# Dilated attention, then routed experts, on one core: query blocks of 64 with two heads in the halves of the array, routing of two batches at a time, and place writes that are not ordered among themselves

## The chip, the cores and the metric

The kernel runs on one core of one Trainium2 chip. The metric is device time in microseconds (us). Three runs of the kernel before gave 985.47, 986.65 and 988.72 us; the median, 986.65 us, is the time before. About 0.3% (3 us) is what a measurement of this kernel can tell from no change.

## What is computed

Eight batches of 576 positions, eight heads of 64 features. A head attends over a causal window: heads 0 to 3 over the last 32 positions, heads 4 to 7 over every fourth of the last 128. The result, with the heads side by side, is x with 512 features per token. Each token has the logits of eight experts and a local gate; where the gate is at least one half, the token takes the expert of the token before it, otherwise that of its largest logit. The expert is two matmuls with a ReLU between.

```python
scores = where(mask, q @ k.T / 8, -1e9);  attn = softmax(scores);  x = attn @ v       # mask by head
logits = x @ w_gate;  local_gate = sigmoid(x @ w_local)
e = argmax(logits[b, s]) if s == 0 or local_gate[b, s] < 0.5 else prev_e               # in order of s
out[b, s] = softmax(logits[b, s])[e] * (relu(x[b, s] @ w1[e]) @ w2[e])                 # w1 512x1024, w2 1024x512
```

## The kernel before

Everything is float32, and each float32 matmul of the program is two passes in the profile. The dilated heads are stored by position modulo 4, so that both kinds of head have a window of 32 neighbours.

**Attention.** The loop over n runs over 32 pairs of heads (four per batch). `scores(n)` (L227) takes six blocks of 96 queries against 128 keys. The two heads of a pair share one matmul of 128 rows: the host lays q out with zeros (`_apart`, L656), 192 columns for a block, so that each head's 64 features meet zeros of the other. VectorE adds the mask out of PSUM (L241), ScalarE takes the exponential (L244). `values(n)` (L277) multiplies the 12 blocks of weights with v, whose last column of ones gives the sums, and VectorE normalises into `x` of the batch (L290 to L292).

**Routing.** After a batch's four pairs `route(b)` (L579) puts nine steps into the list `waiting`; `gap()` runs one of them at each of three places of the loop. They store x to the array `xd` in DRAM (L302, L307), turn x by TensorE (`x_turn`, L317) into `xt`, make the logits (L332, four column tiles of the array side by side), choose the expert (`fresh`, `carry`, `carry_over`, `carry_in`, `choose`) and, in `place` (L429), give each token a place in the table `tab` in DRAM. Eight indirect DMAs of GpSimd (L447) write the pairs of token and gate, `pay`, to the places `pi`, 72 tokens at a time. These write to the same tensor, and the framework orders each behind the one before it. The small tiles of the routing come from a pool of two buffers, and `pay` is written by L426 and L427.

**Experts.** The tokens of an expert fill tiles of 128; there are 43 tiles in all. The first 8 are planned by `table(False)` after five batches, the others by `table(True)` after all eight. A tile gathers its x (`gather`, L539), turns it (`features`, L546, L548), and runs `hidden` (L557, L559) and `output` (L565, L567); L568 scatters the result to the tokens' rows. w1 and w2 of an expert (2 MB each) go into two slots, tile t into slot t % 2, by a conditional load on SyncE's queue (L534) where the expert of tile t differs from that of tile t - 2. `tokens(True)` (L512) is called at tile 5 and needs all of `tab`. The routing of the last batch runs in the gaps of the first tiles.

What sets the order: TensorE runs in the order in which the program is written; the other engines' order is a scheduler's, and each of them works strictly in that order. SyncE issues the loads of q, k, v, the stores of x and the weights, on one queue. GpSimd issues the place writes, the gathers and the result's scatters, on another.

Of the kernel before, what the change touches and what calls it, by code (L numbers as in the profile page):

```python
# [10 lines left out]
F32 = mybir.dt.float32  # L11
BF16 = mybir.dt.bfloat16
I32 = mybir.dt.int32
Act = mybir.ActivationFunctionType
Alu = mybir.AluOpType
AX = mybir.AxisListType
ET = mybir.EngineType
PSUM = bass.MemoryType.PSUM
# [12 lines left out]
QB = 96  # L31
NB = S // QB
KW = QB + WIN
HB = NB // 2

NP = H // 2
UB = 2
NU = NB // UB
VW = DH + 1

TB = 72
NJ = S // TB
NC = 4
LW = 32
# [4 lines left out]
FLOOR = 2.0 ** -100  # L49
CEIL = 80.0 * DH ** 0.5  # L50
# [7 lines left out]


EARLY, FIRST = 5, 8  # L60
assert EARLY * S - E * (P - 1) > (FIRST - 1) * P
# [13 lines left out]
C_TOK = C_CODE + NJ  # L75
C_ROW = C_TOK + NJ
C_COL = C_ROW + NT
C_ALL = C_COL + 1


def constants():

    c = np.zeros((P, C_ALL), np.float32)
    c[:, C_ID:C_TRI] = np.eye(P)
    c[:TB, C_TRI:C_IDX] = np.triu(np.ones((TB, TB)), 1)
    c[:, C_IDX:C_REV] = np.arange(E)
    c[:, C_REV:C_BASE] = E - np.arange(E)
    c[:, C_BASE:C_CODE] = np.arange(E) * CAP * P
    s = np.arange(NJ)[None] * TB + np.arange(P)[:, None]
    c[:, C_CODE:C_TOK] = s * CW + E  # L90
    c[:, C_TOK:C_ROW] = s
    c[:, C_ROW:C_COL] = np.arange(NT)
    c[:, C_COL] = np.arange(P)
    return c


def block_mask(edge=None):

    p = np.arange(QB)[:, None]
    w = np.arange(KW)[None]  # L100
    ok = (w > p) & (w <= p + WIN)
    if edge is not None:
        ok &= ~((p >= edge) & (w - WIN < edge))
    return np.where(ok, 0.0, MASK)


def masks():

    plain = [block_mask(0)] + [block_mask()] * (NB - 1)
    starts = {i // QB: i % QB for i in range(0, S, CI)}  # L110
    dilated = [block_mask(starts.get(i)) for i in range(NB)]
    return np.concatenate([m.T for m in plain + dilated], 1).astype(ml_dtypes.bfloat16)


def query_masks():

    plain = [block_mask(0)] + [block_mask()] * (NB - 1)
    starts = {i // QB: i % QB for i in range(0, S, CI)}
    dilated = [block_mask(starts.get(i)) for i in range(NB)]
    return np.concatenate([np.eye(QB)] + plain + dilated, 1).astype(ml_dtypes.bfloat16)  # L120
# [3 lines left out]
def dilated_attn_locality_moe_kernel(  # L124
    ctx: ExitStack,
    tc: tile.TileContext,
    q: bass.AP,
    k: bass.AP,
# [13 lines left out]
    ones = keep.tile([QB, P], F32, name="ones")  # L142
# [3 lines left out]
    args = (q, k, v, wgl, w1, w2, con, msk, qmk, out, cst, wg, ones)  # L146
# [9 lines left out]
def whole(ctx, tc, exact, bad, q, k, v, wgl, w1, w2, con, msk, qmk, out, cst, wg, ones):  # L156
# [8 lines left out]
    xd = dram.tile([N + 1, D], F32, name="xd")  # L165
    tab = dram.tile([(PADS + 1) * P, 2], F32, name="tab")
    ident = cst[:, C_ID:C_TRI]

    once = pool("once", 1)
    ins = pool("ins", 3)  # L170
    work = pool("work", 6)
    xp = pool("xp", 2)
    sm = pool("sm", 2)
    gp = pool("gp", 3)
    mp = pool("mp", 2)
    banks = pool("banks", 6, space=PSUM)
    pvp = pool("pvp", 1, space=PSUM)

# [5 lines left out]
    rec = once.tile([QB, B * NP, 2, NB], F32, name="rec")  # L184
    loaded = {}

    def load(n):
        qt = ins.tile([P, NB, 2, QB], F32, name="qt")
        kt = ins.tile([P, WIN + S], F32, name="kt")
        vt = ins.tile([P, 2, NB, VW], F32, name="vt")  # L190
        nc.sync.dma_start(out=kt, in_=k[n])
        nc.sync.dma_start(out=qt.rearrange("p i u s -> p (i u s)"), in_=q[n])
        nc.sync.dma_start(out=vt.rearrange("p u i e -> p (u i e)"), in_=v[n])
        loaded[n] = kt, qt, vt

    load(0)
    if not exact:
        mk = once.tile([KW, 2 * NB * QB], BF16, name="mk")
        nc.sync.dma_start(out=mk, in_=msk)
    else:  # L200
        qm = once.tile([QB, QB + 2 * NB * KW], BF16, name="qm")
# [7 lines left out]
    fill = once.tile([P, PADS + 1, 2], F32, name="fill")  # L209
    nc.vector.memset(fill[:, :, 0], NOBODY)  # L210
    nc.vector.memset(fill[:, :, 1], 0.0)
    nc.gpsimd.dma_start(out=tab.rearrange("(p r) c -> p (r c)", p=P), in_=fill.rearrange("p r c -> p (r c)"))
    zero = once.tile([1, D], F32, name="zero")
    nc.vector.memset(zero, 0.0)
    nc.gpsimd.dma_start(out=xd[N:N + 1], in_=zero)
# [3 lines left out]
    def load_first():  # L219

        for i in range(2):
            nc.sync.dma_start(out=w1s[i].rearrange("p m k f -> p (m k f)"), in_=w1[0])
            nc.sync.dma_start(out=w2s[i].rearrange("p m f -> p (m f)"), in_=w2[0])
# [3 lines left out]
    def scores(n):  # L227
# [4 lines left out]
        for c in range(NU):  # L232
            sc = bank([KW, 2, UB, QB], "sc")
            for i in range(UB):
                s = (c * UB + i) * QB
                nc.tensor.matmul(sc[:, :, i], lhsT=kt[:, s:s + KW], rhs=qt[:, c * UB + i],  # L236
                                 start=True, stop=True)
            pr = work.tile([KW, 2, UB, QB], F32, name="pr")
            at = (kind * NB + c * UB) * QB
            flat = pr.rearrange("w u i p -> w u (i p)")  # L240
            nc.vector.scalar_tensor_tensor(  # L241
                flat, sc.rearrange("w u i p -> w u (i p)"), CEIL,
                mk[:, at:at + UB * QB].unsqueeze(1).to_broadcast([KW, 2, UB * QB]), Alu.min, Alu.add)
            nc.scalar.activation(pr, pr, Act.Exp, scale=SCALE)  # L244
            prob[n].append(pr)

    def scores_exact(n):
# [4 lines left out]
        for c in range(NU):  # L252
            sc = bank([QB, UB, 2, KW], "sc")
            first = True
            for i in range(UB):
                s = (c * UB + i) * QB
                at = QB + (kind * NB + c * UB + i) * KW
                for u in range(2):
                    nc.tensor.matmul(sc[:, i, u], lhsT=qm[:, :QB], rhs=qm[:, at:at + KW],
                                     start=first, stop=False, skip_group_check=True)  # L260
                    nc.tensor.matmul(sc[:, i, u], lhsT=qt[:, c * UB + i, u], rhs=kt[:, s:s + KW],
                                     start=False, stop=True, skip_group_check=True)
                    first = False
            top = sm.tile([QB, UB, 2], F32, name="top")
            nc.vector.tensor_reduce(top, sc, axis=AX.X, op=Alu.max, negate=True)
            nc.vector.tensor_scalar_mul(top, top, SCALE)
            ex = work.tile([QB, UB, 2, KW], F32, name="exq", bufs=1)
            pt = bank([KW, 2, UB, QB], "pt")
            for i in range(UB):
                for u in range(2):  # L270
                    nc.scalar.activation(ex[:, i, u], sc[:, i, u], Act.Exp, scale=SCALE, bias=top[:, i, u:u + 1])
                    nc.tensor.transpose(pt[:, u, i], ex[:, i, u], ident[:QB, :QB])
            pr = work.tile([KW, 2, UB, QB], F32, name="pr")
            nc.vector.tensor_copy(pr, pt)
            prob[n].append(pr)

    def values(n, u):  # L277
        b, g = divmod(n, NP)
        vt = loaded[n][2]
        if g == 0 and u == 0:  # L280
            xs[b] = xp.tile([QB, NB, D], F32, name="x")
        if u == 0:
            prob[n].append(pvp.tile([QB, 2, 512], F32, name="pv"))
        ps = prob[n]
        pv = ps[NU][:, :, :NB * VW].rearrange("p u (i e) -> p u i e", i=NB)
        for i in range(NB):
# [410 lines left out]
```

## Time and profile before

| | before |
|---|---|
| runs, median (lowest to highest) | 986.65 us (985.47 to 988.72) |
| profiled execution, own time | 981.2 us |
| its span | 979.0 us |
| TensorE busy | 817.4 us (84%) |
| VectorE busy | 202.0 us (21%) |
| ScalarE / GpSimd busy | 131.3 us (13%) / 148.3 us (15%) |
| bytes moved by DMA | 165.88 MB |

The span runs from the first to the last instruction of the core; 2.2 us of the profiled execution lie outside it. Busy shares are means over a stage of attention, some 325 us, and a stage of experts, the rest, which have different limits. The chain of waits follows the last instruction back to what released each step, so that a wait on it has cost time, and a busy engine off it has not.

### The profile page before, as it was taken

How to read it: one execution, taken by the hardware profiler on the slowest of the kernel's cores; microseconds unless marked ns; L12 is line 12 of the kernel's file. 1: busy time of each engine (PE TensorE's matmuls, PEld its weight loads, DVE VectorE, ACT ScalarE, POOL GpSimd, SP SyncE). 2: the span in 40 equal slices, each digit the busy share in tenths (PEclk: the TensorE clock that was granted, in tenths of full speed). 3: DMA queues.
4: the chain of work that ended last, by engine and by line, in shares of the span. 5: the costliest groups of instructions: out<-in, count | busy, mean ns of one | idle time of the engine just before them, and what ended most of it. 6: DMA issues, size and time to landing. Idle time of an engine off the chain costs nothing.

```text
span 979.0 us, 13125 instructions
## 1 busy us (share of the span) xinstructions
PE 817.4 (84%) x5310; PEld 641.2 (65%) x5310; DVE 202.0 (21%) x639; ACT 131.3 (13%) x263; POOL 148.3 (15%) x158
## 2 busy tenths in 40 slices
PE   6981728283562999599999999999999999999995
PEld 6880628273562776376776777677677677677764
DVE  4561405252433213001001010010100100101000
ACT  2430303030331100000000000000000000000000
POOL 0011111111123222211111111111111111111000
PEclk9995858695977799889999999999999999999998
DMA  8875767482842166558885281731381370820000
GB/s 299 298 225 178 254 212 210 130 214 56 255 92 60 36 212 202 188 192 324 332 320 209 103 306 44 284 124 43 119 291 35 129 284 33 317 99 33 31 1 4
DMA packets 39637, 165.88 MB, mean 169 GB/s; under 512 B 6904, under 2 KB 16391, under 8 KB 33936
## 3 DMA queue, kind: packets, MB, share of 16 engines
q1 hardware_dynamic: 30448, 143.84, 43.3%
q0 software_dynamic: 9120, 21.11, 6.7%
q8 instruction: 44, 0.72, 0.3%
q14 instruction: 25, 0.20, 0.1%
HBM read 242.18 MB, written 21.04 MB: 269 GB/s over the span
## 4 chain that ended last, share of the span: by engine, by line
PE 66%; DMA 26%; issue 4%; DVE 2%; POOL 1%; SPq 0%; POOLq 0%; DVEq 0%
PE hp L557 30%; PE yp L565 29%; DMA tab<-pay,pi 25%; PE sc L236 2%; PE pv L287 2%; PE tp L546 2%; DMA qt<-in_q_dram 1%; POOL tab L447 1%; DVE pr L241 0%; PE tp L317 0%; POOL xg L539 0%; PE kp L437 0%; DVE x L292 0%; DMA tr_late<-tab,ri_late 0%; PE lp L332 0%
## 5 line engine op out<-in xcount | busy, mean ns | idle before, releaser
L557 PEld LDWEIGHTS hp<-xgt,w1s 128*128 128x128 f32 x2752 | 317.5, 194 | 20.2 <-issue 18.2
L557 PE MATMUL hp<-xgt,w1s 128*128 128x128 f32 x2752 | 319.1, 277 | 1.2 <-DVE xgt L548 1.2
L565 PE MATMUL yp<-w2s,h 128*128 128x512 f32 x688 | 302.4, 592 | 0.0
L565 PEld LDWEIGHTS yp<-w2s,h 128*128 128x128 f32 x688 | 127.4, 190 | 144.0 <-issue 144.0
L559 ACT ACTIVATE h<-hp 128x512 f32<-128x512 f32 x86 | 51.4, 597 | 599.4 <-PE hp L557 599.4
L236 PE MATMUL sc<-qt,kt 128*128 128x192 f32 x384 | 86.5, 386 | 25.5 <-DMA qt<-in_q_dram 25.5
L447 POOL DMA_INDIRECT tab<-pay,pi x64 | 59.8, 934 | 308.1 <-DMA tab<-pay,pi 221.0
L236 PEld LDWEIGHTS sc<-qt,kt 128*128 128x128 f32 x384 | 77.2, 229 | 27.7 <-issue 27.6
L567 DVE TENSOR_SCALAR y<-yp,gate 128x512 f32<-128x512 f32 x43 | 32.2, 750 | 271.3 <-PE yp L565 271.3
L568 POOL DMA_INDIRECT out_dram<-y,tok x43 | 43.3, 1006 | 293.5 <-DVE y L567 266.2
L548 DVE COPY xgt<-tp 128x512 f32<-128x512 f32 x43 | 29.7, 690 | 273.1 <-PE tp L546 273.1
L437 PE MATMUL kp<-cum,ones 72*72 72x64 f32 x16 | 3.6, 326 | 96.2 <-DVE cum L415 96.2
L287 PE MATMUL pv<-vt,pr 128*96 128x65 f32 x768 | 78.2, 256 | 0.0
L244 ACT ACTIVATE pr<-pr 128x384 f32<-128x384 f32 x96 | 48.4, 523 | 217.5 <-DVE pr L241 111.1
L287 PEld LDWEIGHTS pv<-vt,pr 128*96 128x96 f32 x768 | 74.8, 173 | 0.4
L539 POOL DMA_INDIRECT xg<-xd,tok x43 | 41.9, 975 | 215.0 <-PE tp L546 199.1
L437 PEld LDWEIGHTS kp<-cum,ones 72*72 72x72 f32 x16 | 2.3, 199 | 97.2 <-DVE cum L415 97.2
L241 DVE SCALAR_TENSOR_TENSOR pr<-sc,mk 128x384 f32<-128x384 f32 x96 | 50.4, 551 | 27.8 <-PE sc L236 18.8
L292 DVE TENSOR_TENSOR x<-pv,rec 96x768 f32<-96x768 f32 x32 | 30.4, 951 | 1.1 <-DVE rec L291 0.4
L546 PE MATMUL tp<-cst,xg 128*128 128x128 f32 x172 | 26.3, 276 | 0.0
L426 DVE TENSOR_SCALAR pay<-cst 72x8 f32<-72x8 f32 x8 | 1.2, 166 | 110.6 <-DMA tab<-pay,pi 110.6
L546 PEld LDWEIGHTS tp<-cst,xg 128*128 128x128 f32 x172 | 20.4, 143 | 0.0
(118 smaller groups left out, 189.4 us busy)
## 6 DMA issues: line engine op xcount, KB each, us to landing
w1s<-in_w_dram SPq DMA_DIRECT2D x45, 2048.0 KB
w2s<-in_w_dram SPq DMA_DIRECT2D x45, 2048.0 KB
qt<-in_q_dram SPq DMA_DIRECT2D x32, 576.0 KB
vt<-in_v_dram SPq DMA_DIRECT2D x32, 390.0 KB
kt<-in_k_dram SPq DMA_DIRECT2D x32, 304.0 KB
xd<-x SPq DMA_DIRECT2D x8, 576.0 KB
xd<-x SPq DMA_DIRECT2D x16, 192.0 KB
xd<-x SPq DMA_DIRECT2D x16, 96.0 KB
```

The lines of the kernel that those rows point to most:

```text
L236: nc.tensor.matmul(sc[:, :, i], lhsT=kt[:, s:s + KW], rhs=qt[:, c * UB + i], start=True, stop=True)
L241: nc.vector.scalar_tensor_tensor(flat, sc.rearrange("w u i p -> w u (i p)"), CEIL, mk[:, at:at + UB * QB].unsqueeze(1).to_broadcast([KW, 2 ...
L244: nc.scalar.activation(pr, pr, Act.Exp, scale=SCALE)
L287: nc.tensor.matmul(pv[:, u, i], lhsT=ps[i // UB][:, u, i % UB], rhs=vt[:, u, i], start=True, stop=True)
L447: nc.gpsimd.indirect_dma_start(out=tab, out_offset=bass.IndirectOffsetOnAxis(ap=pi[:, j:j + 1], axis=0), in_=st["pay"][:, j], in_offset=None)
L539: nc.gpsimd.indirect_dma_start(out=x, out_offset=None, in_=xd if t >= FIRST else xd[:EARLY * S], in_offset=bass.IndirectOffsetOnAxis(ap=of ...
L546: nc.tensor.transpose(tp[:, kk], x[:, kk * P:(kk + 1) * P], ident)
L557: nc.tensor.matmul(hp[:, m], lhsT=w1s[t % 2][:, half * FK // 2 + m, kk], rhs=x[:, kk], start=(kk == 0), stop=(kk == DK - 1))
L559: nc.scalar.activation(ht[t][:, half * FK // 2:(half + 1) * FK // 2], hp, Act.Relu)
L565: nc.tensor.matmul(yp, lhsT=h[:, m], rhs=w2s[t % 2][:, m], start=(m == 0), stop=(m == FK - 1))
L567: nc.vector.tensor_scalar(y, yp, of_tile("gate", t), None, Alu.mult)
L568: nc.gpsimd.indirect_dma_start(out=out, out_offset=bass.IndirectOffsetOnAxis(ap=of_tile("tok", t), axis=0), in_=y, in_offset=None, bounds_ ...
```

## The change

Query blocks are of 64 (nine of them, against 96 keys). q and k come unpadded, in one array and one load per pair. A score matmul has 64 rows: head u of the pair stands in rows 64u to 64u+63 of the array (`tile_position=(u * DH, 0)`) and writes a PSUM bank of its own. A value matmul has 64 columns: head u stands in columns 64u to 64u+63 (`(0, u * QB)`), so that the result has two heads' queries on 128 partitions. VectorE works on units of five and four blocks. The floor under the sums is gone, and the clamp of the scores is done with the mask in the same instruction (maximum, then minimum, where it was minimum, then add).

```diff
-        for c in range(NU):
-            sc = bank([KW, 2, UB, QB], "sc")
...
-                nc.tensor.matmul(sc[:, :, i], lhsT=kt[:, s:s + KW], rhs=qt[:, c * UB + i],
-                                 start=True, stop=True)
+        for a, z in UNITS:
+            sc = scp.tile([P, 2, 512], F32, name="sc")
+            for i in range(a, z):
+                for u in range(2):
+                    h = slice(u * DH, (u + 1) * DH)
+                    nc.tensor.matmul(sc[:KW, u, (i - a) * QB:(i - a + 1) * QB], lhsT=kt[h, i * QB:i * QB + KW],
+                                     rhs=qt[h, i * QB:(i + 1) * QB], start=True, stop=True,
+                                     tile_position=(u * DH, 0))
...
+                    nc.tensor.matmul(pv[u * QB:(u + 1) * QB, i - a], lhsT=pr[:, u, (i - a) * QB:(i - a + 1) * QB],
+                                     rhs=vt[:, u, i], start=True, stop=True, tile_position=(0, u * QB),
+                                     skip_group_check=True)
```

x is kept per two pairs (256 features of a batch) and turned by `turn(m)` in nine transposes of 128. Routing takes two batches at a time: four routes instead of eight, 96 tokens by 12 instead of 72 by 8, seven steps, two gaps per pair. The running count of each expert is one scan instead of eight additions. `pay` lies in the constants, one row of buffers per route, and `pi` has two buffers. The twelve place writes of a route are declared free of order among all place writes; the reads of `tab` wait for all of them.

```diff
-        st["pay"] = pay = sm.tile([TB, NJ, 2], F32, name="pay")
-        nc.vector.tensor_scalar(pay[:, :, 0], cst[:TB, C_TOK:C_ROW], float(b * S), None, Alu.add)
-        nc.vector.tensor_tensor(pay[:, :, 1], mine, total, op=Alu.mult)
+        nc.vector.tensor_tensor(pay[:, g, :, 1], mine, total, op=Alu.mult)
...
-        for j in range(NJ):
-            nc.gpsimd.indirect_dma_start(
+            i = nc.gpsimd.indirect_dma_start(
                 out=tab, out_offset=bass.IndirectOffsetOnAxis(ap=pi[:, j:j + 1], axis=0),
-                in_=st["pay"][:, j], in_offset=None)
+                in_=pay[:, g, j], in_offset=None)
+            for other in scatters:
+                tc.declare_no_dep(i.ins, other.ins, reason="no two tokens have one place")
+            scatters.append(i)
```

x goes to two arrays, `xd[0]` for the plain heads and `xd[1]` for the dilated ones, 128 features (512 bytes) in a piece; a tile gathers two halves, by `tok` and by a third column `pos` of the table. The stores of the first four batches are issued as their tiles are done, the others after the last pairs. Eleven tiles are planned early (from four batches) instead of eight (from five), so that the tiles' order of experts is another; `tokens(True)` is called at tile 8. The experts' tiles take over the memory of the attention's pools, and `tokens(False)` with the first gathers is called behind the last pair instead of two pairs ahead of it. The first weights are loaded at pairs 22 and 25 (slot 0) and 31 (slot 1) instead of all at pair 12.

```diff
+        b, g = divmod(m, 2)
+        to = xd[g][b * S:(b + 1) * S].rearrange("(i q) (u f) -> u q i f", q=QB, u=2)
+        for u in range(2):
+            nc.sync.dma_start(out=to[u], in_=x[u * QB:(u + 1) * QB].rearrange("q i g d -> q i (g d)"))
...
-EARLY, FIRST = 5, 8
+EARLY, FIRST = 2, 11
...
-        if n == 3 * NP:
-            load_first()
-        if n == B * NP - 2:
-            tokens(False)
...
+        if n == NPB - 2:
+            for m in range(KEPT, (n - 1) // 2):
+                store(m)
+        if n in (NPB - 10, NPB - 7):
+            load_first(0, n > NPB - 9)
+        if n == NPB - 1:
+            load_first(1, False)
+            load_first(1, True)
+    for m in sorted(xs):
+        store(m)
+    attention.close()
...
+    tokens(False)
```

Three places show what moves. GpSimd, the place writes (DMASW0 to DMASW7 are the eight semaphores that its DMAs take in turn; a row with none waits for no DMA). Before:

```order
L447 DMA tab<-pay,pi 36992x2 [waits DMASW0_49,DVE_49]
L447 DMA tab<-pay,pi 36992x2 [waits DMASW2_49]
L447 DMA tab<-pay,pi 36992x2 [waits DMASW3_49]
L447 DMA tab<-pay,pi 36992x2 [waits DMASW4_49]
L447 DMA tab<-pay,pi 36992x2 [waits DMASW5_49]
```

The change, the first route:

```order
L474 DMA tab<-cst,pi 36992x4 [waits DMASW3_49,DMAHW5_49,DMASW2_49,DVE_49]
L474 DMA tab<-cst,pi 36992x4 x3
L474 DMA tab<-cst,pi 36992x4 [waits DMASW0_49]
L474 DMA tab<-cst,pi 36992x4 [waits DMASW1_49]
L474 DMA tab<-cst,pi 36992x4 x2
L474 DMA tab<-cst,pi 36992x4 [waits DMASW4_49]
```

Before, each write waits for the semaphore of the one issued just ahead of it; now it waits at most for the write eight places ahead, whose semaphore it takes over.

VectorE, in the second batch's routing, before (`pay` is the tile that the place writes read, `pr` the masked scores):

```order
L427 TENSOR_TENSOR pay<-mine,total 72x8
L292 TENSOR_TENSOR x<-pv,rec 96x2x6x64 [waits DVE_49]
L415 TENSOR_TENSOR cum<-cum,oh 72x8 [waits DVE_49]
L426 TENSOR_SCALAR pay<-cst 72x8 [waits DMASW4_49,DMASW5_49,DMASW3_49,DMASW6_49,DMASW2_49,DMASW7_49,DMASW1_49,DMASW0_49]
L415 TENSOR_TENSOR cum<-cum,oh 72x8 [waits DVE_49] x2
L413 COPY cum<-cum 72x8 [waits DVE_49]
L440 TENSOR_TENSOR pl<-kp,cst 72x64 [waits PE_49]
L441 TENSOR_TENSOR pl<-pl,oh 72x64 [waits DVE_49]
L444 TENSOR_REDUCE pf<-pl 72x8 [waits DVE_49]
L241 SCALAR_TENSOR_TENSOR pr<-sc,mk 128x384 [waits PE_49]
```

The change, the second route:

```order
L451 TENSOR_TENSOR ex<-ex,oh 96x96
L467 TENSOR_TENSOR pl<-kp,cst 96x96 [waits PE_49]
L453 TENSOR_REDUCE mine<-ex 96x12 [waits DVE_49]
L468 TENSOR_TENSOR pl<-pl,oh 96x96 [waits DVE_49]
L454 TENSOR_TENSOR cst<-mine,total 96x12 [waits DVE_49]
L266 SCALAR_TENSOR_TENSOR pr<-sc,mk 96x640 [waits PE_49,Activation_49]
```

L426, which waits for eight DMAs of GpSimd ahead of the next scores, has gone, and no instruction of this route waits for a place write.

TensorE, the end of the attention. Before:

```order
L384 MATMUL last<-cst,run 1x8
L517 MATMUL tt<-cst,tr_early 128x8 x2
L236 MATMUL sc<-qt,kt 128x2x96 x6
L394 MATMUL op<-ones,over 8x1
L287 MATMUL pv<-vt,pr 96x65 x6
L400 MATMUL cp<-cst,run 72x8
L287 MATMUL pv<-vt,pr 96x65 x6
L435 MATMUL kp<-oh,cst 72x64
L437 MATMUL kp<-cum,ones 72x64
L287 MATMUL pv<-vt,pr 96x65 x12
L546 MATMUL tp<-cst,xg 128x128 x4
```

The change:

```order
L261 MATMUL sc<-kq 96x64 x18
L312 MATMUL pv<-vt,pr 64x65 x18
L332 MATMUL tp<-cst,x 128x128 x9
L312 MATMUL pv<-vt,pr 64x65 x18
L332 MATMUL tp<-cst,x 128x128 x9
L358 MATMUL lp<-xt,wg 32x288 x16
L551 MATMUL tt<-cst,tr_early 128x11 x3
L582 MATMUL tp<-cst,xg 128x128 x4
```

The turning of the early table (`tt`), which the first gathers need, stood a pair and a half ahead of the first tile's `tp`; now nothing stands between them.

## Rows read from the trace of the kernel before

**Rows 1.** The page's 40 slices of 24.5 us: bytes moved per second.

```profile
GB/s 299 298 225 178 254 212 210 130 214 56 255 92 60 36 212 202 188 192 324 332 320 209 103 306 44 284 124 43 119 291 35 129 284 33 317 99 33 31 1 4
```

**Rows 2.** The page's chain that ended last, by line.

```profile
PE hp L557 30%; PE yp L565 29%; DMA tab<-pay,pi 25%; PE sc L236 2%; PE pv L287 2%; PE tp L546 2%; DMA qt<-in_q_dram 1%; POOL tab L447 1%; DVE pr L241 0%; PE tp L317 0%; POOL xg L539 0%; PE kp L437 0%; DVE x L292 0%; DMA tr_late<-tab,ri_late 0%; PE lp L332 0%
```

**Rows 3.** Chain of waits in time, attention: start us, us, what.

```profile
11.79 3.90 PE sc L236 x12
...
17.70 2.00 PE sc L236 x12
19.71 2.01 PE pv L287 x24
...
31.76 0.99 PE tp L317 x12
...
36.95 2.15 PE sc L236 x12
...
43.50 3.39 PE sc L236 x12
...
56.96 6.69 DMA tab<-pay,pi
63.94 7.28 DMA tab<-pay,pi
```

**Rows 4.** Waiting engine and releaser: us in total, times, longest us.

```profile
POOL tab L447 <- DMA tab<-pay,pi: 221.0, 54, 7.4
...
DVE pay L426 <- DMA tab<-pay,pi: 110.6, 6, 27.2
ACT pr L244 <- DVE pi L445: 103.7, 6, 25.9
...
PE kp L437 <- DVE cum L415: 96.2, 7, 22.0
...
PE tt L517 <- DMA tr_late<-tab,ri_late: 13.3, 1, 13.3
```

**Rows 5.** Chain of waits in time, experts' tiles.

```profile
324.98 5.89 PE hp L557 x32
...
418.30 8.87 PE hp L557 x64
...
434.47 7.14 PE hp L557 x64
...
448.92 7.14 PE hp L557 x64
...
961.81 6.88 PE yp L565 x16
```

**Rows 6.** Groups of VectorE instructions: busy us, mean ns, idle before.

```profile
L241 DVE SCALAR_TENSOR_TENSOR pr<-sc,mk 128x384 f32<-128x384 f32 x96 | 50.4, 551 | 27.8 <-PE sc L236 18.8 <-DMA mk<-in_msk_dram 7.1 <-PE lt L344 0.5
...
L292 DVE TENSOR_TENSOR x<-pv,rec 96x768 f32<-96x768 f32 x32 | 30.4, 951 | 1.1 <-DVE rec L291 0.4
...
L415 DVE TENSOR_TENSOR cum<-cum,oh 72x8 f32<-72x8 f32 x64 | 9.9, 155 | 0.7
...
L291 DVE RECIPROCAL rec<-rec 96x12 f32<-96x12 f32 x32 | 7.1, 222 | 0.6
```

**Rows 7.** Timeline, last batch's logits: start us, us, engine, line.

```profile
343.69 0.89 PEld L332 LDWEIGHTS lp<-xt,wg 128*32 128x32 f32 x32 [0.76 <-issue]
343.69 1.19 PE L332 MATMUL lp<-xt,wg 128*32 128x144 f32 x32
```

**Rows 8.** DMA view: a queue, and median us to landing.

```profile
q1 hardware_dynamic: 30448, 143.84, 43.3%
...
xg<-xd,tok POOLq DMA_INDIRECT x43, 4.7
```

**Rows 9.** Stretch, us, busy PE, PEld, DVE, ACT, POOL, clock, DMA share, GB/s.

```profile
12.00:42.00 30.00, 28.47 (x265) 27.79 (x265) 17.48 (x48) 12.77 (x28) 0.00 (x0) 1.00 0.88 304
80.00:84.00 4.00, 0.00 (x0) 0.00 (x0) 0.00 (x0) 0.00 (x0) 0.00 (x0) 0.50 1.09 446
```

More of the change, by code (lines that the diff above doesn't have):

```diff
@@ L279, in values @@
         vt = loaded[n][2]
[L280 to L286, printed above, removed]
-            nc.tensor.matmul(pv[:, u, i], lhsT=ps[i // UB][:, u, i % UB], rhs=vt[:, u, i], start=True, stop=True)
-        if u == 0:
-            return
-        nc.vector.tensor_scalar(rec[:, n], pv[:, :, :, DH], FLOOR, None, Alu.max)
@@ new lines, in values, with turn @@
+        del loaded[n]
+    def turn(m):
+        x = xs[m]
+        b, g = divmod(m, 2)
+        if m % (2 * GB) == 0:
+            routes[b // GB] = dict(xt=xtp.tile([P, 2, GS, CH], F32, name="xt"))
+        xt = routes[b // GB]["xt"]
+        w = NB // 3
+        for c in range(3):
+            tp = bank([P, w, 2, QB], "tp")
+            for i in range(w):
+                nc.tensor.transpose(tp[:, i].rearrange("p u q -> p (u q)"),
+                                    x[:, c * w + i].rearrange("p g d -> p (g d)"), ident)
+            s = b % GB * S + c * w * QB
+            nc.scalar.copy(xt[:, g, s:s + w * QB].rearrange("p (i q) u -> p i u q", i=w), tp)
@@ L514, in tokens @@
         nt = NT - FIRST if late else FIRST
-        for c, (what, dtype) in enumerate((("tok", I32), ("gate", F32))):
+        for c, (what, dtype) in enumerate((("tok", I32), ("gate", F32), ("pos", I32))):
             tp = bank([P, nt], "tt")
             nc.tensor.transpose(tp, tr[:, :, c], ident[:nt, :nt])
-            tiles[what, late] = to = once.tile([P, nt], dtype, name=f"{what}{late:d}")
+            tiles[what, late] = to = stage[late].tile([P, nt], dtype, name=f"{what}{late:d}")
             nc.vector.tensor_copy(to, tp)
@@ L537, in gather @@
     def gather(t):
[L538 to L540 removed]
+        xg[t] = x = gp.tile([P, 2, D // 2], F32, name="xg")
+        for g, what in enumerate(("tok", "pos")):
+            nc.gpsimd.indirect_dma_start(
+                out=x[:, g], out_offset=None, in_=xd[g] if t >= FIRST else xd[g][:EARLY * GS],
+                in_offset=bass.IndirectOffsetOnAxis(ap=of_tile(what, t), axis=0))
     def features(t):
[L543 removed]
+        x = xg.pop(t).rearrange("p g f -> p (g f)")
         tp = bank([P, DK, P], "tp")
```

421 lines of the change are left out of this document (211 added, 210 removed).

## The prediction, made before the change was timed

> **What bounds the kernel now.** I read the page's chain by line first [rows 2]: TensorE's expert matmuls (hp and yp) hold 59% of the span, and 25% is a wait for DMAs that write places into `tab`. That is work of 16 bytes a token, so the second number is a serial latency, and the question is where it lies. The chain in order of time answers [rows 3]: up to 37 us it runs pair after pair on TensorE (scores at 17.70, values at 19.71, 4.02 us a pair), and from 57 us it is one place write after another, 6.69 and 7.28 us each. The waits say how that reaches TensorE [rows 4]: GpSimd waits 221.0 us for the preceding write; VectorE stands 110.6 us at `pay`, whose buffer the writes still read; and what is queued behind `pay` on VectorE (the counts for `kp`, `pi`, the next masked scores) holds TensorE 96.2 us at `kp` and ScalarE 103.7 us. So the attention is bound by the chain of places, at about twice its own work. The first expert matmul starts at 324.98 us [rows 5].
>
> From there the tiles are TensorE's: one starts every 14.45 us (434.47 to 448.92) [rows 5]. At tile 5 TensorE waits 13.3 us for `tr_late`, which waits for the last place writes [rows 4], and starts again slowly: 8.87 us for 64 passes against 7.14 [rows 5].
>
> **The experts after the change.** 43 x 14.45 = 621.4 us. The first tile starts behind an idle TensorE: its first 32 passes took 5.89 us where 3.57 is the rate of the later tiles [rows 5], 2.3 more. The seven small routing steps of the last two batches in the first tiles: 1.9. After the last matmul (961.81 + 6.88 = 968.7) the span has 10.3 us of result, check and end; unchanged. Sum 635.9, against 979.0 - 325.0 = 654.0 now. The 13.3 us at `tr_late` go: the last places are issued in tile 1, 12 of them, and even 12 in a line at 7 us would be 84 us, with the table read at tile 8, some 87 us later. Turning the last batch's x leaves the tiles too.
>
> The weights: with eleven early tiles from four batches the order of the tiles' experts, which I worked out from the inputs, asks for 25 loads of 4.19 MB instead of 20, and every tile from 2 to 12 has one. The loads now make 22 x 4.19 = 92 of queue q1's 143.84 MB [rows 8]; the rest is attention. A tile with a load, its gather and its result moves 4.7 MB, or 326 GB/s at 14.45 us. The kernel before has eight such tiles in a row (6 to 13), where the slices show 324, 332 and 320 GB/s [rows 1] and the tiles keep their 14.45 us. So I cost the five loads at nothing; their cover is the 22 us from the moment a slot is free to the matmul that wants it.
>
> **The attention after the change, per pair.** *Scores*: 9 blocks x 2 heads x 2 passes = 36 passes of 64 columns with weights 96 wide. The nearest row is values now: 24 passes of 65 columns with weights 96 wide in 2.01 us, 84 ns each [rows 3]. One after another that is 3.0 us; if the two heads' halves run side by side, 1.5. *Values*: 36 passes with weights 64 wide, 64/96 of 84 = 56 ns: 2.0 us one after another, 1.0 side by side. Do tiles of the array run side by side here? The logits show it [rows 7]: 32 passes of 144 columns in four column tiles take 1.12 us, 35 ns each, where one alone takes 144/128 x 112 = 125 ns by the rate of hp. So streams of column tiles overlap. But their 32 weight loads are busy 0.89 us, 28 ns each, back to back: loads of column tiles came one after another, and 64 columns of load are then 56 ns. I take values at 1.9, near the serial end, and scores at 1.8, near the parallel end, since the two heads' weights come from different partitions.
>
> [...]
>
> [...] *Turning x*: 9 transposes of 128 per two pairs; 12 of 96 took 0.99 us [rows 3], so 0.99 per two pairs, 0.5 a pair. *Logits*: 32 passes of 288 columns per eight pairs, twice 1.12 us, 0.3 a pair. TensorE: 1.8 + 1.9 + 0.5 + 0.3 + 0.4 = **4.9 us a pair**, bounds 3.7 and 6.2.
>
> What could be above that? *VectorE*: from 551 ns at 384 elements and 951 at 768 [rows 6], 1.04 ns an element and 151 fixed. Masked scores 640 and 512: 0.82 + 0.68; normalising 320 and 256: 0.48 + 0.42; two reciprocals 0.44; sum 2.85, and some 30 small instructions of 0.2 us a route, 0.75 a pair: 3.6. The scan for eight additions of 155 ns saves 1.1 us a batch off the path. *DMA*: q and k 0.61 MB and v 0.45 in place of 1.30; a store adds 0.30 a pair in the first half: 1.35 MB, 4.4 us at the 304 GB/s of the stretch where TensorE was the limit, and 3.0 at 446, the most that a stretch shows [rows 9]. The stores are in 512-byte pieces, which no row prices; I keep 4.4, still under 4.9, and it is next in line. *ScalarE* exponentiates 1152 columns a pair as before, in two instructions instead of three, and copies as many turned columns. [...]
>
> *Stalls of a route*: between two score groups there were 6.55 us with routing steps (36.95 to 43.50) against 4.02 without [rows 3], 2.5 us more. I take two of those, 5 us, for each of three routes inside the loop: 15.
>
> *Places*: 36 of the 48 fall into the attention; GpSimd issues them in about 1 us each with nothing behind them until the first gather, and VectorE no longer stands at `pay`. Costed at nothing; if they were still in a line, see the rivals.
>
> *Stores moved to the end and first weights*: six stores (3.5 MB) and slot 1's weights (4.2 MB) stand on SyncE's queue at the end, 8.9 MB with the last stores, 29 us at 304 GB/s, begun some 20 us ahead of the first tile. Tile 0 uses slot 0, loaded long before, and tile 1 starts 14.45 us later: hidden, with some 5 us to spare. *Hand-over*: `tt`, the copies of tok and pos, two gathers of 1 us issue and 4.7 us to landing [rows 8], transposes and copy, behind the last values, turn and logits (5 us): 14 us open, where before the gathers were early.
>
> **The sum.** Second pair's scores at 10 us (11.79 now [rows 3], with less to load ahead of it); 31 x 4.9 = 151.9; last values 2; stalls 15; hand-over 14: first tile at 193 us instead of 325. Plus 635.9 is a span of 828.8, and with 2.2 us outside it 831. The profiled execution (981.2) was 5.45 us under the median of the runs (986.65); with as much, **836 us**.
>
> **Rivals.**
> - *The halves take turns* in both kinds of matmul: 6.2 us a pair, 31 x 1.3 = 40 more, and longer stalls: 881 us. For it: the loads of rows 7. Against it: the streams of rows 7.
> - *Everything runs side by side* and VectorE is the limit, at 3.6 and some waiting, 3.9 a pair: 31 less, stalls 7 less: 798. [...]
> - *Weights bind the early tiles*: at 300 GB/s, 15.7 us for each of 11 tiles, 14 more: 850. Against it: rows 1.
> - *The places are still in a line* in effect, through the semaphores that they share: 36 of them from about 75 us on, at 3.8 us (25% of the span over 64 writes [rows 2]) to 7 us [rows 3], and the first gathers stand behind them on GpSimd; first tile at 220 to 335 us: 863 to 978. Against it: the order of the instructions, where a write waits for the eighth ahead of it.
> - *Slower than before*: smaller pieces leave gaps, the clock stays at 0.50 as it did behind idle stretches [rows 9], and the halves take turns: 12.4 us a pair, 31 x 7.5 = 232 more, first tile after that at some 440 us: 1080. It decides from 9.7 us a pair on ((986.65 - 7.65 - 635.9 - 41)/31). Against it: a TensorE with 95% work had its full clock in rows 9.
>
> **How the numbers follow.** Forecast 0.55, halves in turns 0.20, side by side 0.13, weights 0.05, places in a line 0.04, slower 0.03. Range 798 to 885: both bounds of the pair's cost with the weights' case, leaving out the last two and part of the forecast's tails. All but the last case, and the upper end of the places' case, are faster by far more than 0.3% (3 us, about what a measurement can tell): faster 0.95, same 0.01, slower 0.04.
>
> **What would show it.** Right: no wait of VectorE for a place write; scores about every 4.9 us in an unrouted stretch; `hp` from about 193 us; no wait at `tr_late`; tiles of 14.45 us from 2 to 12. A score group near 3.0 us or 1.5 us decides between the first two rivals, the clock row the last. The forecast is wrong if pairs come slower than 6.2 us, if tiles stretch with DMA near its limit, or if the chain still lists places.

## The result, and the profile after

The changed kernel takes **878.37 us** (median of four, 875.66 to 881.49) against 987.64 (985.47 to 988.72) of the kernel before: ratio 0.8897, 95% interval 0.8861 to 0.8933. The forecast was 836.0, the range 798 to 885: faster as said, inside the range, 42 us above the forecast.

| | forecast | after (profiled) | difference |
|---|---|---|---|
| second pair's scores to the last values | 10 to 178.9 us | 9.5 to 213.75 us | +34.9 |
| hand-over to the first `hp` | 14 | 12.0 (225.72) | -2.0 |
| experts to the end of the span | 635.9 | 648.2 | +12.3 |
| span | 828.8 | 873.9 | +45.1 |

The page of the changed kernel, its chain of waits by engine and by line, answers to [rows 2]:

```profile
PE 87%; issue 4%; DMA 4%; DVE 2%; another core or an unknown queue 1%; ACT 0%; POOL 0%; POOLq 0%; DVEq 0%; ACTq 0%
PE hp L593 35%; PE yp L601 34%; PE sc L261 7%; PE pv L312 5%; DMA kq<-in_qk_dram 3%; PE tp L332 2%; PE tp L582 2%; PE lp L358 2%; DVE pr L266 1%; DMA xg<-xd,tok 1%; DVE x L317 0%; PE lt L370 0%; DVE rec L316 0%; DVE y L603 0%
```

No place write is on the chain any more, as forecast. New is a releaser that the profile can't name (1%). The waits (waiting instruction, releaser: us, times, longest) say where, in place of [rows 4]:

```profile
DVE pr L266 <- remote: 43.9, 4, 16.2
PE pv L312 <- issue: 24.4, 28, 1.8
ACT h L595 <- remote: 12.1, 1, 12.1
PE sc L261 <- DMA kq<-in_qk_dram: 9.2, 5, 5.3
PE tp L582 <- DMA xg<-xd,tok: 4.8, 1, 4.8
```

"remote" means that no event in the trace explains the release; "issue" is idle time in which the engine waited for nothing that the profile shows. VectorE stands four times before masked scores, 43.9 us, and TensorE 24.4 us in 28 short gaps between value matmuls. In the timeline of the first of these stalls (start, us, engine; the last column is idle time and its releaser) the pieces stand side by side:

```profile
80.88 1.75 PE L261 MATMUL sc<-kq 64*96 64x64 f32 x36 [1.00 <-DMA kq<-in_qk_dram]
81.85 0.91 POOL L474 DMA_INDIRECT tab<-cst,pi  x1 [0.31 <-issue]
82.55 0.45 PE L312 MATMUL pv<-vt,pr 96*64 96x65 f32 x7
83.06 0.91 POOL L474 DMA_INDIRECT tab<-cst,pi  x1 [0.30 <-issue]
83.16 0.27 PE L312 MATMUL pv<-vt,pr 96*64 96x65 f32 x1 [0.16 <-issue]
85.42 0.82 DVE L266 SCALAR_TENSOR_TENSOR pr<-sc,mk 96x640 f32<-96x640 f32 x1 [5.88 <-remote]
...
92.21 0.91 POOL L474 DMA_INDIRECT tab<-cst,pi  x1 [0.30 <-issue]
92.35 0.38 PE L312 MATMUL pv<-vt,pr 96*64 96x65 f32 x2 [1.13 <-issue]
95.16 0.71 PE L312 MATMUL pv<-vt,pr 96*64 96x65 f32 x8 [0.22 <-issue]
95.45 0.69 DVE L266 SCALAR_TENSOR_TENSOR pr<-sc,mk 96x512 f32<-96x512 f32 x1 [9.21 <-remote]
```

The scores of 80.88 took 1.75 us, yet VectorE got them at 85.42 and 95.45. TensorE did a value group, 1.27 us elsewhere, in 13 us, one to eight passes at a time. All the while GpSimd issued place writes 1.21 us apart, 78.1 to 93.1 us. The other stalls lie in the same place: writes 131.5 to 145.8, stall to 148.4; writes 186.0 to 200.3, stall to 203.6; and in tile 2, where TensorE runs on but its results are taken late:

```profile
260.57 0.94 POOL L474 DMA_INDIRECT tab<-cst,pi  x1 [0.30 <-DVE pi L472]
262.03 3.65 PEld L593 LDWEIGHTS hp<-xe,w1s 128*128 128x128 f32 x32
266.15 3.60 PE L601 MATMUL yp<-w2s,h 128*128 128x512 f32 x8
274.92 0.60 ACT L595 ACTIVATE h<-hp 128x512 f32<-128x512 f32 x1 [12.14 <-remote]
275.09 0.91 POOL L474 DMA_INDIRECT tab<-cst,pi  x1 [0.31 <-issue]
275.56 2.93 PE L601 MATMUL yp<-w2s,h 128*128 128x512 f32 x3 [5.81 <-ACT h L595]
```

In each stall the granted clock falls to 0.50, and a stretch at that level follows: 84 to 102 us, 138 to 158, 194 to 212 and 276 to 280 (the score group of 95.80 us took 3.15 us). The windows (columns: PE, weight loads, DVE, ACT, POOL busy; granted clock; DMA share; GB/s) answer to [rows 9]:

```profile
12.00:42.00 30.00, 28.56 (x497) 26.51 (x494) 15.07 (x37) 11.63 (x19) 0.00 (x0) 1.00 0.91 271
42.00:110.00 68.00, 54.23 (x817) 45.73 (x815) 30.61 (x95) 21.36 (x38) 11.02 (x12) 0.75 0.76 208
110.00:175.00 65.00, 51.09 (x806) 41.15 (x806) 31.87 (x119) 20.31 (x38) 11.85 (x13) 0.82 0.75 226
175.00:240.00 65.00, 47.01 (x527) 38.54 (x526) 21.05 (x74) 14.10 (x26) 20.47 (x22) 0.76 0.84 233
```

They show 1.00 in the first window and 0.75 to 0.82 in the others, means of stretches at 1.00 and at 0.50. The stalls are not the only cause of the lower level: a score group, 1.75 us at the full clock, was slow before the first place write too. (In the first window the 1.00 holds for the second half alone: the trace has no clock record ahead of 28 us, and the score groups of 15.38 and 20.60 us took 3.15 us.)

```profile
50.43 3.15 PE L261 MATMUL sc<-kq 64*96 64x64 f32 x36
```

The theory to test (A): place writes that GpSimd issues in a row stall TensorE. The rival (B): transfer queues full of loads and of the 512-byte stores of x do.

### The profile page after: what moved, and what is told of

Same layout as the page of the kernel before. It is cut to its first block, busy times and chain, and to the rows that moved or that the text cites. A ratio compares the mean times of both kernels' runs of the same rounds, so it can differ in the third digit from the quotient of the medians.

```text
span 873.9 us, 14741 instructions
## 1 busy us (share of the span) xinstructions
PE 801.1 (92%) x6248; PEld 606.4 (69%) x6248; DVE 169.9 (19%) x454; ACT 120.1 (14%) x207; POOL 173.7 (20%) x187
## 4 chain that ended last, share of the span: by engine, by line
PE 87%; issue 4%; DMA 4%; DVE 2%; another core or an unknown queue 1%; ACT 0%; POOL 0%; POOLq 0%; DVEq 0%; ACTq 0%
PE hp L593 35%; PE yp L601 34%; PE sc L261 7%; PE pv L312 5%; DMA kq<-in_qk_dram 3%; PE tp L332 2%; PE tp L582 2%; PE lp L358 2%; DVE pr L266 1%; DMA xg<-xd,tok 1%; DVE x L317 0%; PE lt L370 0%; DVE rec L316 0%; DVE y L603 0%
## 5 line engine op out<-in xcount | busy, mean ns | idle before, releaser
L593 PEld LDWEIGHTS hp<-xe,w1s 128*128 128x128 f32 x2752 | 315.9, 193 | 20.4 <-issue 19.9
L593 PE MATMUL hp<-xe,w1s 128*128 128x128 f32 x2752 | 317.2, 276 | 1.2 <-issue 0.8
L261 PE MATMUL sc<-kq 64*96 64x64 f32 x1152 | 70.2, 283 | 13.2 <-DMA kq<-in_qk_dram 9.2
L312 PE MATMUL pv<-vt,pr 96*64 96x65 f32 x1152 | 59.5, 261 | 24.4 <-issue 24.4
L261 PEld LDWEIGHTS sc<-kq 64*96 64x96 f32 x1152 | 64.9, 195 | 20.0 <-DMA kq<-in_qk_dram 8.0
L474 POOL DMA_INDIRECT tab<-cst,pi x48 | 43.9, 914 | 161.3 <-DVE pi L472 107.8
L312 PEld LDWEIGHTS pv<-vt,pr 96*64 96x64 f32 x1152 | 50.8, 171 | 31.5 <-issue 29.2
L266 DVE SCALAR_TENSOR_TENSOR pr<-sc,mk 96x640 f32<-96x640 f32 x64 | 48.1, 753 | 108.4 <-remote 43.9
L269 ACT ACTIVATE pr<-pr 96x640 f32<-96x640 f32 x64 | 43.6, 684 | 128.0 <-DVE pr L266 118.6
L574 POOL DMA_INDIRECT xg<-xd,pos x43 | 40.8, 948 | 13.1 <-issue 11.6
```

Source lines behind the costliest of these rows:

```text
L261: nc.tensor.matmul(sc[:KW, u, (i - a) * QB:(i - a + 1) * QB], lhsT=kt[h, i * QB:i * QB + KW], rhs=qt[h, i * QB:(i + 1) * QB], start=True, ...
L266: nc.vector.scalar_tensor_tensor(pr[:, :, :w], sc[:KW, :, :w], -CEIL, mk[:, at:at + w].unsqueeze(1).to_broadcast([KW, 2, w]), Alu.max, Alu ...
L269: nc.scalar.activation(pr[:, :, :w], pr[:, :, :w], Act.Exp, scale=SCALE)
L312: nc.tensor.matmul(pv[u * QB:(u + 1) * QB, i - a], lhsT=pr[:, u, (i - a) * QB:(i - a + 1) * QB], rhs=vt[:, u, i], start=True, stop=True, t ...
L474: i = nc.gpsimd.indirect_dma_start(out=tab, out_offset=bass.IndirectOffsetOnAxis(ap=pi[:, j:j + 1], axis=0), in_=pay[:, g, j], in_offset=None)
L574: nc.gpsimd.indirect_dma_start(out=x[:, g], out_offset=None, in_=xd[g] if t >= FIRST else xd[g][:EARLY * GS], in_offset=bass.IndirectOffse ...
```

## Experiments: the places

**At most three place writes under way.** A write waits for the third ahead of it:

```diff
-            for other in scatters:
+            for other in scatters[:-3] + scatters[1 - 3:]:
                 tc.declare_no_dep(i.ins, other.ins, reason="no two tokens have one place")
+            if j >= 3:
+                tc.add_manual_dep(i.ins, scatters[-3].ins.name, SYNC, reason="at most 3 at once")
```

> Edit: a place write waits for the third place write ahead of it, so that at most three are under way; nothing else. Theory A (places): VectorE's waits of 5.9, 9.2, 12.6 and 16.2 us at the masked scores and ScalarE's 12.1 us at h in tile 2 each begin when some three to five of a route's 12 place writes are under way, and end when the last of them begin to move, so they come from the number of place writes under way. Then these five waits (56 us) go for the most part, the clock stays nearer to 1.00, the first hp starts at 170 to 190 us in place of 225.7 and the time is 820 to 845. Theory B (full queues): they come from the loads and the 512-byte stores of x alone; then the waits stay and the time is 870 to 885. Theory C (the places themselves are now late): with a landing of some 14 us each, the 12 writes of the second route end some 50 us after they begin, the early table is late, and the first hp stays near 220 although the waits go.

850.09 us, ratio 0.8659 (0.8619 to 0.8699), just above A's range. No wait on "remote" is left, as A said: tile 2 takes 14.70 us in place of 23.49, and the last values end at 177.4 us, 36 earlier. But the first `hp` comes at 205.33, between A and C, by a wait of C's kind: the gathers of the first tiles now stand behind the third route's places on GpSimd.

```profile
176.08 1.27 PE L312 MATMUL pv<-vt,pr 96*64 96x65 f32 x36
195.93 0.91 POOL L474 DMA_INDIRECT tab<-cst,pi  x1 [2.13 <-DMA tab<-cst,pi]
197.15 1.00 POOL L576 DMA_INDIRECT xg<-xd,tok  x1 [0.30 <-DMA w2s<-in_w_dram]
205.33 5.47 PE L595 MATMUL hp<-xe,w1s 128*128 128x128 f32 x32 [0.83 <-issue]
```

**One at a time**, the order of the kernel before, with the rest of the change (no `declare_no_dep`):

> Edit: every place write waits for the one ahead of it, as before the change; nothing else. Prices the unordered writes. Theory A: none of the five waits is left, but the second route's 12 writes, begun at some 120 us at 7 us (as before) to 14 us each, end at 205 to 290 us, the early table after them, the first hp at 220 to 310 us: 870 to 960 in all. Theory B: the waits stay, and the first hp is at 260 us or later: 910 or more.

899.02 us, 0.9156 (0.9108 to 0.9204); first `hp` at 240.43, no stall, all inside A's ranges. TensorE waits 33.5 us for the early table.

```profile
POOL tab L474 <- DMA tab<-cst,pi: 181.6, 42, 7.7
PE tt L551 <- DMA tr_early<-tab,ri_early: 33.5, 1, 33.5
```

So leaving the order away is worth 2.6% of the time before as the change does it (0.9156 to 0.8897), and 5.0%, 48.9 us on the same chip, with a limit of three.

**No places at all** (`for j in range(0)`, and the table is filled with zeros instead of the number that stands for no token):

> Leaves out the 48 place writes: every tile then gathers token 0, and only the stretch up to the first hp is read. Theory A: the four waits at the masked scores go, the first hp starts at 170 to 185 us. Theory B: it starts at 220 to 230 us, with the waits where they were.

Attention as under A: no stall, last values end at 176.3 us. The first `hp`, at 199.74, lies between both forecasts, by waits at the hand-over:

```profile
183.41 14.23 SPq L341 DMA_DIRECT2D xd<-x  x4
191.39 0.66 PE L580 MATMUL tp<-cst,xg 128*128 128x128 f32 x2 [9.82 <-DMA xg<-xd,tok]
199.74 2.47 PE L591 MATMUL hp<-xe,w1s 128*128 128x128 f32 x10 [6.15 <-DMA w1s<-in_w_dram]
```

SyncE reaches the weights of tiles 0 and 1 only at 199.52, behind the last stores. B falls for the stalls: loads and stores of this stretch are all there, the stalls are not.

**Pauses** between the writes, which stay unordered (GpSimd's order is also the program's here, and no longer the scheduler's):

```diff
             scatters.append(i)
+            for _ in range(3):
+                nc.gpsimd.memset(rest, 0.0)
```

> Edit: after every place write GpSimd fills a scratch tile three times (1.5 to 3 us estimated, no row has it), so that place writes stay unordered but are issued some 3 us apart instead of 1.2; GpSimd keeps the program's order. Theory A1 (rate): TensorE is stalled by place writes issued back to back; then the four waits at the masked scores and the one at h go as with three at once, and the time is 845 to 865. Theory A2 (number): it is stalled by how many are under way; since a write lands some 4 to 15 us after its issue when the loads fill the engines, three to five are under way here too, and at least two of the five waits stay, 20 us or more in sum.

870.91 us (two runs), 0.8899 (0.8842 to 0.8956): above A1's range, and no faster than the changed kernel (0.8897). The writes come 2.79 us apart, and no wait on "remote" is left. But then only some two were under way (counted from their packets), so A2's premise did not arise: rate and number are not told apart here. What the stalls cost comes back elsewhere: the granted clock is 0.66 in the mean of 110 to 175 us (0.87 with three at once), the last values end at 194.4 us, the first `hp` comes at 220.32, behind writes that last to 212.5, and tile 4 takes 27.97 us.

**The unordered writes alone, in the kernel before:** the same `declare_no_dep` among its 64 writes.

> The kernel before with one part of the change alone: its place writes (64, of 8 bytes for each of 72 tokens) are not ordered among themselves, and the reading of the table waits for all. Theory A: the chain of places held that kernel's attention at twice its own work, 325 us to the first hp; without it the first hp starts at 185 to 235 us, the wait at the late table goes too, and the time is 840 to 890, so the blocks of 64 and the halves of the array are worth little beside it. Theory B: the smaller blocks and the halves carry the gain; then this kernel stays above 930. Bursts of eight place writes may stall TensorE as twelve did, 3 to 10 us a batch, inside the first range.

929.17 us, 0.9501 (0.9459 to 0.9544): A's range ended at 890, and the time is at B's bound of 930. The first `hp` comes at 282.4 us, not at A's 185 to 235. The old kernel now shows waits of the same kind, so they need neither the halves of the array nor the blocks of 64:

```profile
DVE pay L427 <- DMA tab<-pay,pi: 53.2, 6, 12.2
ACT h L567 <- remote: 26.5, 2, 17.1
ACT xt L321 <- remote: 25.8, 7, 6.1
```

`pay` still waits 53.2 us for the writes that read it, 110.6 before [rows 4]. Of the change's 11%, this part alone gives 5.0 and all but this part 8.4 (one at a time); the two do not add up.

## Experiments: the halves and the transfers

**Halves in turn:** the loop over the two heads is put outside that over the blocks, in scores and values.

```diff
-            for i in range(a, z):
-                for u in range(2):
+            for u in range(2):
+                for i in range(a, z):
```

> Edit: in scores and values the loop over the two heads is the outer one, so that successive matmuls are of one half of the array; same instructions in another order. If successive matmuls run side by side only when they alternate between the halves, a score group takes 3.0 us at the full clock instead of 1.75 and a value group 2.0 instead of 1.27, 2 us a pair, 64 us if TensorE sets the pair's time (940 in all), 20 to 40 us if other engines hide half of it (900 to 920). If the order does not matter, the groups keep 1.75 and 1.27 us and the time is 875 to 885.

898.34 us, 0.9135 (0.9095 to 0.9174). At the full clock, first two rows, of this kernel:

```profile
36.99 2.41 PE L261 MATMUL sc<-kq 64*96 64x64 f32 x36
39.33 1.78 PE L312 MATMUL pv<-vt,pr 96*64 96x65 f32 x36
96.74 4.28 PE L261 MATMUL sc<-kq 64*96 64x64 f32 x36
```

and of the changed one:

```profile
31.05 1.75 PE L261 MATMUL sc<-kq 64*96 64x64 f32 x36
32.72 1.27 PE L312 MATMUL pv<-vt,pr 96*64 96x65 f32 x36
```

Alternating gives 0.66 us of the scores and 0.51 of the values, 1.2 a pair, not the 2 expected. Yet the last values end some 59 us later than with three at once (236.1 against 177.4). For 32 pairs at the full clock the order alone would give 37 us (1.17 a pair); this TensorE also runs long at half its clock, from 80 to 120 us at 0.50 although it is busy for all of that time:

```profile
60.00:80.00 20.00, 18.54 (x226) 14.83 (x222) 9.52 (x36) 6.60 (x13) 0.00 (x0) 0.84 0.68 195
80.00:100.00 20.00, 20.00 (x186) 19.00 (x186) 7.32 (x25) 4.24 (x7) 6.21 (x7) 0.50 0.57 136
100.00:120.00 20.00, 20.00 (x196) 19.08 (x195) 5.95 (x14) 4.97 (x8) 4.82 (x6) 0.50 0.93 190
```

And against A: twelve writes a route, 1.21 us apart, some four under way as in the changed kernel, and **no stall** in any of the four routes. So a row of place writes is not enough for one. Nor is the order of the matmuls the missing condition in every case: tile 2 runs the same instructions in both kernels, beside the fourth route's row of writes and with the transfer engines as busy (a share of 0.86 from 286 to 306 us here, 0.86 from 255 to 266 us in the changed kernel, up to its stall). Here it took 14.70 us from `hp` to `hp`, there 23.49:

```profile
289.96 3.76 PE L593 MATMUL hp<-xe,w1s 128*128 128x128 f32 x32
297.79 7.03 PE L601 MATMUL yp<-w2s,h 128*128 128x512 f32 x16
299.52 0.92 POOL L474 DMA_INDIRECT tab<-cst,pi  x1 [0.30 <-issue]
304.66 7.31 PE L593 MATMUL hp<-xe,w1s 128*128 128x128 f32 x64
```

**The same with the first half's stores of x made twice**, to fill the queues:

> Halves in turn, which issued its 12 place writes a route 1.2 us apart like the changed kernel and yet had none of the stalls, with every store of x of the first half made twice as in stores twice. If the stall takes a row of place writes and transfer queues that are full (in halves in turn the engines moved 108 to 164 GB/s around the first route's writes, in the changed kernel 208 in the mean of 42 to 110 us), the first route's row now meets full queues and VectorE shows a wait of 5 us or more there with no releaser that the profile names. If the order of the matmuls keeps it away, or full queues play no part, there is none, as before.

895.96 us (one run), some four of the first route's 12 writes under way, and no wait on "remote". This does not settle the question for the first route, since the premise was met in part only: the engines' share was 0.65 in the 10 us ahead of the row (90 to 100 us) and 0.74, then 1.24, during it, where the changed kernel had 1.00 ahead of its own (70 to 78 us). For tile 2, where halves in turn had neither other matmuls nor a smaller share of the engines (0.86 in both) than the changed kernel, neither of the two is the condition.

**Stores twice, with three at once:**

> Edit on top of three at once: in the first half every store of x is made twice, the second time into a spare array; 4.7 MB more in 17 pairs. If the pairs are bound by the DMA engines (1.35 MB a pair at the 232 to 285 GB/s of those slices), the score group of pair 17 starts 15 to 19 us later than with three at once (92.4 us) at 107 to 112 us; if by TensorE or VectorE, within 4 us of it.

870.26 us (one run; 0.889 of the kernel before). Pair 17 starts at 106.0 us against 92.4, 13.6 later: below the forecast for pairs wholly bound by transfers, far above 4. From 60 to 100 us the engines' share is 1.02 and 1.04, and they move no more than this:

```profile
60.00:80.00 20.00, 18.03 (x306) 13.57 (x305) 11.79 (x48) 7.30 (x14) 0.00 (x0) 0.94 1.02 274
80.00:100.00 20.00, 15.57 (x208) 14.12 (x206) 7.83 (x22) 6.87 (x12) 5.85 (x7) 0.66 1.04 248
```

So without stalls the pairs of the first half are for the most part bound by the transfers.

## Experiments: a better hand-over

**An early start:** on top of three at once, tokens and gathers of tiles 0 to 2 ahead of the third route's places; `weights` of tiles 0 and 1 ahead of the last 16 stores.

```diff
+    def begin():
+        tokens(False)
+        for t in range(3):
+            gather(t)
...
+        if g == EARLY:
+            waiting.insert(-1, begin)
```

> Edit on top of three at once: the tokens of the early tiles and the gathers of tiles 0 to 2 come ahead of the third route's place writes, and SyncE asks for the weights of tiles 0 and 1 ahead of the last 16 stores of x. With three at once the last values ended at 177.1 us and the first hp started at 205.3, 28 us later, 20.8 of them a wait of TensorE for xg, whose gathers GpSimd issued only at 197 us, behind the third route's places. Theory A: the hand-over is a matter of order, so the first hp starts at 182 to 188 us, tile 0 is no longer cold (2 us), and the time is 824 to 833. Theory B: it is the backlog of stores and first weights in the DMA engines (287 to 346 GB/s in that stretch); then tile 0 or tile 1 waits for its weights or for xg instead, and the time stays at 842 to 852.

849.24 us, 0.8683 (0.8631 to 0.8735): no gain, inside B's range. The last values end late, at 201.4 us, and the first `hp` follows at 208.69. Six gathers in a row bring TensorE's gaps back, though these are few (the two below are 1.4 us); the clock was low for longer, 0.69 in the mean of 110 to 150 us and 0.53 from 175 to 200 us:

```profile
181.40 0.95 POOL L576 DMA_INDIRECT xg<-xd,tok  x1 [0.30 <-issue]
181.98 0.49 PE L312 MATMUL pv<-vt,pr 96*64 96x65 f32 x3 [0.47 <-issue]
182.65 0.94 POOL L576 DMA_INDIRECT xg<-xd,pos  x1 [0.30 <-issue]
183.39 0.38 PE L312 MATMUL pv<-vt,pr 96*64 96x65 f32 x2 [0.92 <-issue]
```

**One tile early** (gathers of tiles 1 and 2 behind a place write of the third route; by the kernel's numbers the sixth and the tenth, not the fourth and the eighth that the expectation names):

> As the early start, but only tile 0 is gathered ahead of the third route's place writes; the gathers of tiles 1 and 2 wait for the fourth and the eighth of them. In the early start six gathers in a row stood on GpSimd from 175 to 184 us, and TensorE had gaps of the stall's kind there (pair 29 took 11.4 us). Theory A (software transfers issued in a row stall TensorE, whatever they are): without that row the pairs keep their pace, the last values end at 175 to 190 us, the first hp follows 6 to 9 us later, and the time is 822 to 838. Theory B (what is won at the hand-over is lost to the stores and first weights): last values and first hp stay at 200 and 209 us, 843 to 852.

846.45 us, 0.8650 (0.8591 to 0.8710). The first `hp` comes at 197.70, better than 205.33; tile 0 takes 19.82 us, with TensorE's gaps at 202 to 206 us, during another row of places and gathers. The last values end at 191.2 us and the time is in B's range; within the intervals it is no better than three at once.

**Three deep** (`kq` three buffers, `ins` four, `xt` one, `load(n + 3)`):

> As one tile early, with q, k and v loaded three pairs ahead in place of two (one buffer more for kq and for vt, one fewer for xt). Theory A (short gaps in the transfers): TensorE's 12 to 14 us of waits for kq and part of the half-clock stretches behind them go, the DMA share of 42 to 160 us comes up to 1.0, and the time is 6 to 14 us under one tile early. Theory B (the bytes): the transfers are at their limit, so waits move from kq to vt or to later pairs, and the time is within 4 us of it.

840.47 us, 0.8572 (0.8522 to 0.8622), 6 us under one tile early, its intervals just overlapping, so A is not shown. The windows 12 to 42 and 42 to 110 us have a DMA share of 1.03 and 1.02, as A said; but of TensorE's waits for kq (10.7 us with one tile early) 7.9 us are left, and from 110 to 150 us the clock stood at 0.52 (0.72 with one tile early). It has the lowest time of this study, 3.2% of the time before under the changed kernel (0.8897 to 0.8572).

**Two at once**, on top of that:

> As three deep, with at most two place writes under way instead of three. Three deep still had gaps of TensorE of the stall's kind at 202 to 207 us, where eight software transfers followed each other on GpSimd 1.2 us apart (193.5 to 204.5 us). Theory A (a row of software transfers on GpSimd stalls TensorE): with two at once the row is shorter, tile 0 takes 14.5 to 16 us instead of 21.8, and the time is 3 to 8 us under three deep (832 to 838). Theory B: the places are now the later ones, the early table and the third route's places come 10 to 20 us later, tile 0 or the late table waits, and the time is 840 to 860.

842.53 us, 0.8598 (0.8559 to 0.8637): tile 0 is 15.16 us, as A said, but TensorE waits 15.7 us for the early table, as B said, and tile 5 takes 21.66 us. No gain.

## Where the prediction was right, and where it was off

**The term that failed is *Places*, "costed at nothing".** The writes cost no engine a wait of its own, as argued; but issued in a row they stalled TensorE and its releases. Without any of them the last values come at 176.3 us instead of 213.75, 37 us; tile 2 took 23.49 us against 14.70 with three at once, 9 more. Together that is as much as the 45 us by which the span was missed; the other differences (13.2 us behind the last matmul for 10.3, a hand-over 2 us shorter than forecast) nearly cancel. Removing the stalls brought less: with three at once the span is 29.5 us shorter (844.4 for 873.9), because the hand-over grew. That the time stayed inside the range is luck: the upper end was made of the pair's cost and slow weights, and a stall was in none of the cases.

**The signs.** No wait of VectorE for a place write, no wait at `tr_late` and tiles of 14.45 us came as named, but for tile 2 and for tile 7 (15.45). The first `hp` at 193 us did not come, and in the mean, routing and stalls included, pairs stood 6.5 us apart (9.54 to 212.25), past the 6.2 that was to show the forecast wrong.

**Pair by pair** the sum was right by luck: without places the last values ended at 176.3, for 178.9 forecast, but the parts were others. A pair needs less of TensorE than 4.9 us: values took 1.27 us where I took 1.9, scores 1.75 for 1.8, and three unrouted pairs came 3.7 us apart (27.94 to 39.09), near the rival "side by side". No run shows the 0.4 us a pair that is the last term of the 4.9: the values began at 32.72 us, no later than the end of the scores before them (31.05 + 1.75 = 32.80). Then the transfers bound most pairs, which I had "next in line" at 4.4 us by a rate of 304 GB/s: the changed kernel's windows with the 512-byte stores show 271 and 208 at a share of 0.91 and 0.76, and with the stores doubled it is 274 and 248 at 1.02 and 1.04. 1.35 MB at 265, an estimate between these two, is 5.1 us.

**The rivals.** "Halves take turns" is out: 1.75 and 1.27 us against 2.41 and 1.78 in turn. The values, at 1.27, are nearer to the parallel end (1.0) than to the serial one (2.0), next to which I had put them. "Weights bind the early tiles" is out: tiles 3 to 6 kept 14.45 us with a load each. "Places in a line" is out for the changed kernel. "Slower" did not come, but part of its mechanism is real: a TensorE busy for 20.00 of 20.00 us at 0.50 (halves in turn, 80 to 120 us) breaks the argument that 95% work keeps the clock, and the changed kernel's own clock was 0.75 to 0.82 in the mean of its windows from 42 us on.

**Hand-over.** 12.0 us for 14, but not as I had counted it: the last stores, which I had beside the first tiles, had the third stall to drain in (221 GB/s at a share of 1.03 from 186 to 203 us). That this made it short is argued, not shown. Without stalls it took 23.4 us (no places, where the stores and the first weights are not "hidden": 9.8 us of waits for `xg`, 6.2 for `w1s`) and 28.0 us (three at once, with the gathers behind the places).

**Experts.** Tiles of 14.45 us hold, no wait at `tr_late`, five more loads free.

**Open.** What turns a row of software transfers into a stall. Places one at a time, limited to three, in pauses or left out have no stall, and the old kernel's free places have it; a row of gathers, or of places and gathers together, brings TensorE's gaps even under the limit of three. But halves in turn issues the same rows of places without a stall, in tile 2 beside the very same instructions. In the stalled stretches the trace also misses records: beside 5,382 packets of four bytes it holds 4,346 semaphore updates by transfers in the changed kernel (from 78 to 96 us 59 beside 274), 5,365 with three at once, 5,332 with halves in turn; that each such packet should have its update is my reading of these counts. Loss and stall do not always go together: with pauses, where no stall is left, it holds 4,645. Every execution listed here has its span and clock on record, and none was made without recording. So it is open whether recording has a part in the stall, and with it whether the kernel loses this time where nothing is recorded.

## What to carry to other kernels

Work that no engine waits for can still slow one, as the place writes did here (37 us in the attention, 9 in tile 2): when writes are freed of their order, look for releases that no event explains, and limit how many are under way before giving the freedom up (limiting to three beat both the free and the ordered version here, 0.8659 against 0.8897 and 0.9156). When a term that bounded a stage shrinks, price the next one by a rate measured on its own transfers (here 248 to 274 GB/s with the 512-byte stores made twice, where I had taken 304), and look at what the emptied time had been hiding.

## What the runs showed of the hardware

- Twelve indirect writes of 96 x 16 bytes, 1.21 us apart: in the changed kernel each of the four rows came with a stall (VectorE and ScalarE stood 5.88 to 16.2 us ahead of TensorE's results, with no releaser in the trace); in halves in turn the same rows came with none.
- Two heads' matmuls in halves of the array, alternating: 36 passes in 1.75 us (scores) and 1.27 us (values); half by half (halves in turn) 2.41 and 1.78, at the full clock.
- TensorE busy for 20.00 of 20.00 us was granted 0.50 of its clock, twice in a row (halves in turn, 80 to 120 us).
